# Left-over tokens on full 128-row matmuls, and new priorities, in an attention and token-mixer kernel

## The chip, the cores and the metric

The kernel runs on one core of one Trainium2 chip. The metric is the device time of one execution in microseconds, the median of several runs. The profile is of one execution.

## The reference

Inputs are q, k and v of 4 batches, 8 heads, 576 tokens and 64 channels a head, with a small position bias from a two-layer function of relative position, and the weights of a mixer block.

```
scores = q @ k.T / 8 + bias(i, j, head)       # 576 x 576 for each of 32 heads
attn   = softmax(scores) ; o = attn @ v        # o: 576 x 64 a head
x      = o with the 8 heads side by side       # batch, 576, 512
h      = relu(x.T @ w_tok1) @ w_tok2           # mixes the 576 tokens (256 hidden)
u      = x + h.T
out    = u + relu(u @ w_ch1) @ w_ch2           # mixes the 512 channels (1536 hidden)
```

## The kernel before

**Units.** Attention and token mixing are done for a pair of heads of one batch at a time: 4 pairs x 4 batches are 16 units. Within a unit the 576 queries are cut into 4 chunks of 128 and a left-over of 64. In the fifth chunk the left-over queries of both heads of the pair stand together: head 0 in rows 0 to 63, head 1 in rows 64 to 127.

**A chunk's steps.** *scores* (L666): four float32 products of 64 rows for each head into a PSUM `pair`. *biased* (L670, VectorE): adds the bias and finds the row maximum. *exp* (L684, ScalarE). Then the numerators are turned: *flip* (L703, TensorE transposes of 512 columns into a PSUM `bank`), *flip_hi* (L706, ScalarE) and *flip_lo* (L710, VectorE) write them as two float16 parts, high and low. What is left of a chunk after two flips goes another way: high part, low part on GpSimd, and a DMA transpose on the SP queue (L722). *back* (L746 to L748) multiplies with v: for each head 5 blocks of keys, and for each block three products (high x high, high x low, low x high), so 30 products of 64 or 65 columns. The column of ones beside v gives the sum of each row. *norm* (guard L767, reciprocal L771, division L780) writes chunks 0 and 1, chunks 2 and 3, and the left-over into the tile `x` (128 x 5 x 128), and so frees the PSUM bank of those backs.

**The left-over before.** Its back takes 64 columns of the turned numerators as weights (the head's own half) and writes to 64 PSUM rows: `r`, rows 0 to 63 for an even batch, 64 to 127 for an odd one. So both heads stand side by side on the same 64 rows.

**Token mixing.** When all five parts of `x` are there, they are split into high and low (L308, L323). *mix1* (L796 to L798) is 2 x 5 x 3 products of 128 columns: 5 blocks of tokens, the last with 64 rows. *relu* (L815, L816). *mix2* (L805 to L807) is 5 x 2 x 3 products of 128 columns; the last block has 64 output columns and goes to the rows `r`. Two residual instructions (L819 for 128 x 512, L821 for 64 x 128) add to `x`, and two stores (L825, L827) put the result into DRAM tensors `um` and `ul`.

**Channel mixing.** u is read back in 18 tiles of 128 tokens, turned, and multiplied: *chan1* (L968 to L970) in 5 blocks, *chan2* (L998 to L1000). The 24 weight pieces are loaded as 64-bit words and decoded into two float16 parts on VectorE, GpSimd and ScalarE (L556 to L571) while attention runs and after it.

**What sets the order.** Every step is an entry of a plan: which engines can do it, an estimated cost, what it follows, which buffers it takes and frees. A list scheduler (`Plan.order`) emits the steps: it finds the engine that can start a step first, and among the steps that can start within `SLACK` (0.097) of that moment it takes the one with the smallest due time. Due times are `BASE + 5 * TICK * unit + TICK * chunk + DUE[kind]`. The emitted order is fixed in the program; each engine runs its own part in that order, with waits for what it needs. The bias is made first, in 36 blocks (L423, L425, L441, L447), and goes through DRAM into the buffers from which L670 reads it.

Of the kernel before, what the change touches and what calls it, by code (L numbers as in the profile page):

```python
# [26 lines left out]
NCH = 4  # L27
# [9 lines left out]
TICK = 2.35  # L37
BASE = 67.64
# [16 lines left out]
DUE = {'blk': 29.05,  # L55
       'blkn': 0.67,
       'rect': -81.27,
       'bmm': -146.83,
       'over': -7.76,
       'put': -41.17,  # L60
       'bl': -22.15,
       'bln': 15.56,
       'sums': -79.57,
       'sumsn': 0.87,
       'meas': -52.82,
       'measn': -1.79,
       'measw': 98.18,
       'measwn': 6.48,
       'amax': 56.12,
       'scales': 48.16,  # L70
       'scalet': -63.64,
       'scalec': -167.78,
       'fill': 239.74,
       'fill1': 213.34,
       'tok': 90.83,
       'tokn': 2.6,
       'dec1': 47.92,
       'dec2': -2.25,
       'dec3': -65.12,
       'dec4': 33.12,  # L80
       'dec5': -14.78,
       'load_k': -23.79,
       'load_q': 70.61,
       'load_v': -135.93,
       'prep_k': -68.51,
       'prep_kl': -48.97,
       'prep_q': 82.92,
       'prep_ql': 1.69,
       'prep_v': -126.84,
       'prep_vh': -4.6,  # L90
       'prep_vl': 125.82,
       'scores': 26.19,
       'biased': 82.41,
       'top': 2.07,
       'exp': -41.11,
       'hi': -98.5,
       'lo': -23.53,
       'flip': 29.87,
       'fliphi': 24.58,
       'flip2': 1.74,  # L100
       'fliplo': 11.27,
       'turn': -7.48,
       'back': -24.67,
       'norm': 83.98,
       'mix0': -57.52,
       'mix1': 39.31,
       'relu': -78.51,
       'mix2': -80.52,
       'mix2b': -120.9,
       'store': 48.6,  # L110
       'w1': 22.4,
       'w1n': 11.84,
       'U0': -13.72,
       'U0n': -3.2,
       'U1n': -19.84,
       'U1': -42.9,
       'U2': 133.32,
       'Un': 3.09,
       'U3': 35.03,
       'U4': 250.78,  # L120
       'u1': -106.99,
       'u2': -102.94,
       'u3': 58.75,
       'u4': 8.97,
       'u5': 73.75,
       'G': 114.15,
       'G0': 71.27,
       'G0n': 7.22,
       'g1': -6.35,
       'g2': 90.55,  # L130
       'ur': 190.4,
       'w2m': 20.95,
       'w2mn': 5.39}
# [9 lines left out]
class Step:  # L143
# [5 lines left out]
    def __init__(self, on, due, do, take, free, use, port):  # L149
        key = next(iter(on))  # L150
        self.wire, self.gate = (on[key] if key in "DQX" else 0.0), key == "X"
        on = {"Q": {"A": 0.1}, "X": {"D": 0.0}, "D": {"D": 0.0}}.get(key, on)
        self.on = {e: x if isinstance(x, float) else x[0] for e, x in on.items()}
        self.shy = {e: 0.0 if isinstance(x, float) else self.grid(x[1]) for e, x in on.items()}
        self.due, self.do, self.take, self.free, self.port = self.grid(due), do, take, free, port
        self.bank = [h for h in {*take, *free, *use} if h.kind in ("pair", "bank")]
        self.next, self.left, self.ready, self.start, self.end = [], 0, 0.0, None, None


class Plan:  # L160
# [5 lines left out]
    def add(self, on, due, do, after=(), take=(), free=(), use=(), port=False):  # L166

        s = Step(on, due, do, take, free, use, port)
        for p in after:
            if p is not None:  # L170
                p.next.append(s)
                s.left += 1
        for h in free:
            h.users += 1
        self.steps.append(s)
        return s

    def order(self):
        room = {k: [(0.0, i) for i in range(n)] for k, n in self.rooms.items()}
        at = {"V": 6.9, "A": 6.8, "P": 4.3, "T": 8.0, "D": 2.1, "-": 0.0}  # L180
        made = wire = port = 0.0
        ready = {e: [] for e in at}
# [9 lines left out]
        while len(out) < len(self.steps):  # L192
            best = None
            for e, steps in ready.items():
                first, can = None, []
                for s in steps:
                    t = max(at[e], s.ready, *(h.busy[0] + (0.0 if h.busy[1] == e else 0.15) for h in s.bank))
                    if e == "P" or e == "V" and s.port:
                        t = max(t, port)
                    for h in s.take:  # L200
                        if not room[h.kind]:
                            break
                        t = max(t, min(room[h.kind])[0])
# [17 lines left out]
            cost = s.on[e]  # L221
            s.start, s.engine = t, e
# [27 lines left out]
def attention_mixer(ctx, tc, qT, kT, v, cst, lg, ident, wt1, wt2, wc1, wc2, out, dump=None):  # L250
# [71 lines left out]
    def less(e, o, x, y):  # L322
# [12 lines left out]
           *((wt2[:, a:a + 1, x:x + 288], 288) for a in range(2) for x in (0, 288))]  # L335
# [11 lines left out]
    with tc.manual_schedule():  # L347
# [12 lines left out]
        st["w2"] = [tld.tile([128, 2, S], F16, name="wt2" + x) for x in "hl"]  # L360
# [69 lines left out]
        for n, (c, o) in enumerate([(c, o) for c in range(NCH + 1) for o in range(8 if c < NCH else 4)]):  # L430
# [23 lines left out]
            m = add({"T": 1.15}, t + DUE["bmm"], mm, after=rs, take=[ph], free=[hs])  # L454
# [122 lines left out]
        for i in range(7):  # L577
# [5 lines left out]
            def part(i=i, x=0):  # L583
                a, b = st["w1"][x], st["w2"][x]
                return ((a[:, 0:2], a[:, 2:4], a[:, 4:5], *(b[:, p:p + 1, y:y + 288] for p in range(2) for y in (0, 288)))[i]
# [35 lines left out]
        def unit(u):  # L621
# [6 lines left out]
            r = slice(64 * (b % 2), 64 * (b % 2) + 64)  # L628

# [19 lines left out]
            for c in range(NCH + 1):  # L649
# [4 lines left out]
                for h in range(2 if c < NCH else 1):  # L654
# [20 lines left out]
                    s = lead = chain("scores", add({"T": 0.6 if c < NCH else 0.66}, t + DUE["scores"], scores, after=[*ready, *bias_in[hp, c], lead if h else None], take=[ph, z] if h == 0 else [ph], free=[hk, hq]))  # L675
# [22 lines left out]
                for i in range(groups):  # L698
# [13 lines left out]
                    s = chain("flip", add({"T": 0.51}, t + DUE["flip"] + DUE["flip2"] * i, flip, after=exps[:i + 1], take=[tb, fb], free=[z]))  # L712
# [16 lines left out]
                def back(e, c=c, t2=t2, ta=ta, hb=hb, m=wn // 128):  # L729
# [4 lines left out]
                    if c < NCH:  # L734
                        q = slice(0, 128)
                        blk = [[(n, n) for n in range(5)], [(n + 1, n) for n in range(4, 9)]]
                        w = [slice(0, 128)] * 2
                    else:
                        q = r
                        blk = [[(n + 5 * h, n) for n in range(5)] for h in range(2)]  # L740
                        w = [slice(0, 64), slice(64, 128)]
                    for h in range(2):
                        for i, (n, t) in enumerate(blk[h]):
                            lh, ll = th[t][:, w[h]], tl[t][:, w[h]]
                            o = ps[q, h, 0:D + 1]
                            PE.matmul(out=o, lhsT=lh, rhs=vh[:, n, 0:D + 1], start=(i == 0), stop=False)  # L746
                            PE.matmul(out=ps[q, h, 0:D], lhsT=lh, rhs=vl[:, n, :], start=False, stop=False)  # L747
                            PE.matmul(out=o, lhsT=ll, rhs=vh[:, n, 0:D + 1], start=False, stop=(i == 4))  # L748

                backs.append(chain("back", add({"T": 1.02}, t + DUE["back"], back, after=[*turned_s, v3, *set_ok, *backs[-1:]], take=[hb] if c in (0, 2) else [],  # L750
# [6 lines left out]
                def view(c=c, hb=hb, hr=hr):  # L757
# [4 lines left out]
                    ps = banks[hb.i][r, 320:480].rearrange("p (c h d) -> p c h d", c=1, h=2)  # L762
                    return ps, rc[r, 0:1], x[r, 4:5].rearrange("p c (h d) -> p c h d", h=2), [64, 1, 2, D]
# [9 lines left out]
                def norm3(e, view=view):  # L773
                    ps, rc, xo, sh = view()
                    if e == "A":
                        for i in range(sh[1]):
                            for h in range(2):
                                A.activation(out=xo[:, i, h], in_=ps[:, i, h, 0:D], func=ACTF.Copy, scale=rc[:, i, h])
# [10 lines left out]
            def mix1(e):  # L789
                (w1h, w1l), (xh, xl) = st["w1"], st["xh"]  # L790
                ps = banks[b1.i].rearrange("p (t c) -> p t c", t=4)
                for t in range(2):
                    for c in range(5):
                        p = slice(0, 128) if c < 4 else r
                        w = slice(t * 128, (t + 1) * 128)
                        PE.matmul(out=ps[:, t], lhsT=w1h[p, c, w], rhs=xh[p, c], start=(c == 0), stop=False)  # L796
                        PE.matmul(out=ps[:, t], lhsT=w1h[p, c, w], rhs=xl[p, c], start=False, stop=False)
                        PE.matmul(out=ps[:, t], lhsT=w1l[p, c, w], rhs=xh[p, c], start=False, stop=(c == 4))  # L798

            def mix2(e):  # L800
                (w2h, w2l), (hh, hl) = st["w2"], st["hh"]
                ps, pl = banks[b2.i].rearrange("p (s c) -> p s c", s=4), banks[b1.i][r, 256:384]
                for o, w in [(ps[:, s], slice(s * 128, (s + 1) * 128)) for s in range(4)] + [(pl, slice(512, S))]:
# [10 lines left out]
            s3 = add({"T": 2.1}, t + DUE["mix1"], mix1, after=[s2, *wt_s[:3]], take=[b1], free=[hx])  # L814
# [3 lines left out]
            s6 = add({"T": 1.98}, t + DUE["mix2"], mix2, after=[s5, *wt_s[3:]], take=[b2], free=[hh], use=[b1])  # L818
            s7 = add({"V": 0.67}, t + DUE["mix2b"], lambda e: V.scalar_tensor_tensor(  # L819
                out=x()[:, 0:4], in0=p2(), scalar=c_tm, in1=x()[:, 0:4], op0=ALU.mult, op1=ALU.add), after=[s6], free=[b2])  # L820
            s8 = add({"V": 0.27}, t + DUE["mix2b"], lambda e: V.scalar_tensor_tensor(  # L821
                out=x()[r, 4], in0=banks[b1.i][r, 256:384], scalar=c_tm[r], in1=x()[r, 4], op0=ALU.mult, op1=ALU.add), after=[s6], free=[b1])
# [4 lines left out]
                add(wire("store", 0.09), t + DUE["store"], lambda e: ENG[e].dma_start(out=u_l[b // 2][r, cs], in_=x()[r, 4]), after=[s8], free=[xh_])]  # L827
# [245 lines left out]
def lay_out(q, k, v, w1, b1, w2, moe_w_tok1, moe_w_tok2, moe_w_ch1, moe_w_ch2):  # L1073
    import numpy as np

    def heads(x):
# [24 lines left out]
        "wt1": wt1.transpose(1, 0, 2), "wt2": t2.reshape(2, 128, S).transpose(1, 0, 2),  # L1101
# [18 lines left out]
```

## Time and profile before

| | |
|---|---|
| timed runs | 712.2, 712.88, 715.33 us; median 712.88 |
| span of the profiled execution, first to last instruction | 709.6 us |
| instructions | 16671 |
| TensorE busy | 660.5 us, 93% |
| VectorE, ScalarE, GpSimd busy | 469.2 (66%), 375.0 (53%), 162.9 us (23%) |
| mean granted TensorE clock | 0.990 |

The profiled execution has no separate time of its own beside its span; 712.88 - 709.6 = 3.3 us is what the median holds more. Busy time of an engine counts an instruction from start to end; matmuls overlap, so for TensorE the distance from one start to the next tells more than the duration of one. A tile of TensorE is written rows*columns of the weights: 128*64 is 128 rows and 64 columns.

### The profile page before, as it was taken

What the parts mean: (1) busy time and instruction counts of PE and PEld (TensorE: products, weight loads), DVE (VectorE), ACT (ScalarE), POOL (GpSimd) and SP (SyncE); (2) the same over time, 40 slices, a digit from 0 to 9 for tenths busy, and PEclk for the clock granted to TensorE, in tenths of its full rate; (3) what the DMA queues carried; (4) which work ended last, traced back from release to release, by engine and by line L of the source; (5) the groups of instructions that cost most, each with busy time, mean ns of one, the idle gap of its engine ahead of it and who ended that gap; (6) DMA issues with size and microseconds to landing.
All of it is one profiled execution on the core that took longest, in us unless ns stands there. A gap on an engine that the chain in (4) does not pass through costs nothing. (4 is left out here: it accounts for less than half of the span.)

```text
span 709.6 us, 16671 instructions
## 1 busy us (share of the span) xinstructions
PE 660.5 (93%) x6612; PEld 391.8 (55%) x6612; DVE 469.2 (66%) x1164; ACT 375.0 (53%) x726; POOL 162.9 (23%) x226
## 2 busy tenths in 40 slices
PE   5776779999999999999999999999999999999997
PEld 2322246676667767776767776444444444446443
DVE  5788788987889999999898777579851022112110
ACT  4667769766787787777877653345531022012010
POOL 0121025332354544453323100013430000000000
PEclk9999999999999999999999999999999999999999
DMA  9878867889756596644452248967623220121021
GB/s 337 332 253 284 280 232 224 245 232 242 237 153 181 132 260 182 177 122 115 135 117 61 49 99 213 296 178 183 181 55 120 60 59 1 29 62 29 19 85 31
DMA packets 86814, 111.42 MB, mean 157 GB/s; under 512 B 46928, under 2 KB 56400, under 8 KB 86736
## 3 DMA queue, kind: packets, MB, share of 16 engines
q1 hardware_dynamic: 72048, 70.90, 35.6%
q10 hardware_dynamic: 14688, 39.46, 17.5%
q8 instruction: 52, 0.85, 0.5%
q14 instruction: 26, 0.21, 0.1%
HBM read 80.31 MB, written 20.05 MB: 141 GB/s over the span
## 5 line engine op out<-in xcount | busy, mean ns | idle before, releaser
L666 PE MATMUL pair<-kk,qq 64*128 64x288 f32 (+1 forms) x640 | 107.6, 454 | 8.6 <-DVE mx L670 5.9
L684 ACT ACTIVATE z<-z,mx 128x576 f32<-128x576 f32 x144 | 110.3, 775 | 6.4 <-DVE mx L691 2.6
L670 DVE CUSTOM_DVE_ANT_0 z<-pair,slots 128x576 f32<-128x576 f32 x144 | 108.4, 757 | 7.6 <-PE pair L666 6.2
L710 DVE TENSOR_TENSOR t2a<-bank,t2a 128x512 f16<-128x512 f32 x144 | 98.3, 687 | 16.4 <-ACT t2a L706 16.0
L706 ACT ACTIVATE t2a<-bank 128x512 f16<-128x512 f32 x144 | 84.4, 588 | 42.3 <-PE bank L703 35.6
L703 PE MATMUL bank<-id,z 128*128 128x128 f32 x576 | 92.7, 285 | 4.6 <-ACT z L684 2.9
L1009 DVE SCALAR_TENSOR_TENSOR o<-bank,crow,ur 128x512 f32<-128x512 f32 x18 | 13.5, 751 | 104.2 <-PE bank L1000 104.2
L703 PEld LDWEIGHTS bank<-id,z 128*128 128x128 f32 x576 | 60.8, 141 | 36.8 <-issue 13.6
L746 PE MATMUL bank<-vh,t2a 128*128 128x65 f16 (+1 forms) x704 | 75.7, 196 | 0.7 <-ACT t2a L706 0.7
L746 PEld LDWEIGHTS <-t2a 128*128 128x128 f16 (+1 forms) x704 | 65.0, 99 | 19.6 <-issue 12.3
L747 PE MATMUL bank<-vl,t2a 128*128 128x64 f16 (+1 forms) x704 | 75.0, 193 | 0.0
L748 PE MATMUL bank<-vh,t2a 128*128 128x65 f16 (+1 forms) x704 | 74.6, 194 | 0.0
L968 PE MATMUL bank<-slots 128*128 128x384 f16 (+1 forms) x192 | 67.8, 353 | 0.8 <-DVE t2a L710 0.8
L323 POOL TENSOR_TENSOR p<-z,p 128x128 f16<-128x128 f32 x80 | 36.6, 459 | 138.1 <-ACT p L308 111.5
L970 PE MATMUL bank<-slots 128*128 128x384 f16 (+1 forms) x192 | 67.7, 353 | 0.0
L969 PE MATMUL bank<-slots 128*128 128x384 f16 (+1 forms) x192 | 67.7, 353 | 0.0
L747 PEld LDWEIGHTS <-t2a 128*128 128x128 f16 (+1 forms) x704 | 65.8, 101 | 1.0 <-issue 0.8
L748 PEld LDWEIGHTS <-t2a 128*128 128x128 f16 (+1 forms) x704 | 65.9, 100 | 0.1
L441 PE MATMUL pair<-slots 128*32 128x288 f32 x576 | 48.5, 455 | 14.6 <-ACT slots L447 13.6
L425 DVE TENSOR_SCALAR slots<-slots 128x576 f32<-128x576 f32 x108 | 51.9, 548 | 15.1 <-PE pair L441 14.9
L666 PEld LDWEIGHTS pair<-kk,qq 64*128 64x128 f32 (+1 forms) x640 | 42.8, 175 | 33.8 <-issue 12.4
L990 ACT ACTIVATE ur<-ur,sc 128x512 f32<-128x512 f32 x18 | 13.0, 720 | 79.2 <-DMA ur<-um 65.1
(171 smaller groups left out, 1404.5 us busy)
## 6 DMA issues: line engine op xcount, KB each, us to landing
raw<-wc SPq DMA_DIRECT2D x48, 512.0 KB, 4.4
bd<-slots ACTq DMA_DIRECT2D x36, 288.0 KB, 4.0
kk<-kT ACTq DMA_DIRECT2D x16, 576.0 KB, 5.1
qq<-qT ACTq DMA_DIRECT2D x16, 576.0 KB, 5.9
slots<-bd SPq DMA_DIRECT2D x16, 576.0 KB, 6.1
tv<-v ACTq DMA_DIRECT2D x16, 320.0 KB, 3.6
slots<-v SPq DMA_DIRECT2D x8, 640.0 KB, 11.6
um<-x SPq DMA_DIRECT2D x16, 256.0 KB, 3.4
```

Of the source, the lines that this page charges most:

```text
L666: PE.matmul(out=o[:, n, 0:i], lhsT=qq[w, q0:q0 + m], rhs=kk[w, k0:k0 + i], start=True, stop=True)
L670: V.tensor_tensor_reduce(out=st["z"][z.i][:, o].rearrange("p (n j) -> p n j", n=2), in0=pairs[ph.i][:, :, 0:i], in1=(bias_m[hp][:, c, h, : ...
L684: A.activation(out=zz, in_=zz, func=ACTF.Exp, bias=mx_t[z.i][:, 2 + h:3 + h], scale=0.125)
L703: PE.transpose(banks[tb.i][:, n * 128:(n + 1) * 128], st["z"][z.i][:, 512 * i + n * 128:512 * i + (n + 1) * 128], id32)
L706: A.activation(out=st["t2a"][h.i][:, 0:4].rearrange("p n q -> p (n q)"), in_=banks[tb.i], func=ACTF.Copy)
L710: V.tensor_tensor(out=x[:, 512:1024], in0=banks[tb.i], in1=x[:, 0:512], op=ALU.subtract)
L746: PE.matmul(out=o, lhsT=lh, rhs=vh[:, n, 0:D + 1], start=(i == 0), stop=False)
L747: PE.matmul(out=ps[q, h, 0:D], lhsT=lh, rhs=vl[:, n, :], start=False, stop=False)
L748: PE.matmul(out=o, lhsT=ll, rhs=vh[:, n, 0:D + 1], start=False, stop=(i == 4))
L968: PE.matmul(out=ps[:, 0:n], lhsT=w[0][:, c], rhs=uh[:, c], start=(c == 0), stop=False)
L969: PE.matmul(out=ps[:, 0:n], lhsT=w[0][:, c], rhs=ul[:, c], start=False, stop=False)
L970: PE.matmul(out=ps[:, 0:n], lhsT=w[1][:, c], rhs=uh[:, c], start=False, stop=(c == 3))
```

## The change

The left-over back now takes all 128 columns as weights for each head, so it computes for both heads' queries with each head's v, on 128 PSUM rows; only the block on the diagonal (rows 0 to 63 for head 0, 64 to 127 for head 1) is used. Division, residual and store take the two diagonal blocks one by one. In `x` the fifth part is therefore block-diagonal, with zeros beside it that were written once. mix1 uses all 128 rows of it (the last 64 rows of the first weights stood in both halves already). mix2 computes 128 output rows for the left-over, with the last 64 columns of the second weights put in twice, so that tile is 640 wide in place of 576.

The scheduler now charges `DRAIN` when TensorE goes on to a step of another tile shape, and a refill of 0.055 for flips after one; costs of TensorE's steps are set anew; and all due times, `TICK` and `BASE` are new.

```diff
-TICK = 2.35
-BASE = 67.64
+DRAIN = 0.095
+ROWS64, ROWS64X2, COLS32 = ("64x128", 0.1), ("64x64", 0.1), ("128x32", 0.1)
+TICK = 3.49
+BASE = 15.749
...
-       'put': -41.17,
+       'put': 21.218,
-       'scores': 26.19,
-       'biased': 82.41,
+       'scores': 59.169,
+       'biased': 76.486,
-       'flip': 29.87,
+       'flip': 64.91,
-       'back': -24.67,
-       'norm': 83.98,
+       'back': -707.069,
+       'norm': 410.436,
-       'mix1': 39.31,
+       'mix1': 48.311,
-       'mix2': -80.52,
+       'mix2': -338.728,
-       'w1': 22.4,
-       'w1n': 11.84,
+       'w1': 556.16,
+       'w1n': -19.871,
...
+                    if e == "T" and s.mode != mode:
+                        t = max(t, at[e] + DRAIN)
...
-       for ... in range(2) for x in (0, 288)    # pieces of the second token weights
+       for ... in range(2) for x in (0, 320)
...
-                            lh, ll = th[t][:, w[h]], tl[t][:, w[h]]
-                            o = ps[q, h, 0:D + 1]
-                            PE.matmul(out=o, lhsT=lh, rhs=vh[:, n, 0:D + 1], start=(i == 0), stop=False)
...
+                            o = ps[:, h, 0:D + 1]
+                            PE.matmul(out=o, lhsT=th[t], rhs=vh[:, n, 0:D + 1], start=(i == 0), stop=False)
...
+                    elif c == NCH:
+                        for h, w in enumerate(half):
+                            V.tensor_scalar(out=xo[w, 0, h], in0=ps[w, 0, h, 0:D], scalar1=rc[w, 0, h], scalar2=None, op0=ALU.mult)
...
-                        p = slice(0, 128) if c < 4 else r
-                        PE.matmul(out=ps[:, t], lhsT=w1h[p, c, w], rhs=xh[p, c], start=(c == 0), stop=False)
+                        PE.matmul(out=ps[:, t], lhsT=w1h[:, c, w], rhs=xh[:, c], start=(c == 0), stop=False)
...
-                ps, pl = banks[b2.i]..., banks[b1.i][r, 256:384]
-                for o, w in [... for s in range(4)] + [(pl, slice(512, S))]:
+                ps, pl = banks[b2.i]..., banks[b1.i][:, 256:384]
+                for o, w in [... for s in range(4)] + [(pl, slice(512, 640))]:
...
+            def mixed_left(e):
+                for h, w in enumerate(half):
+                    o = x()[w, 4, 64 * h:64 * h + 64]
+                    V.scalar_tensor_tensor(out=o, in0=banks[b1.i][w, 256 + 64 * h:320 + 64 * h], scalar=c_tm[w], in1=o, op0=ALU.mult, op1=ALU.add)
+            def store_left(e):
+                for h, w in enumerate(half):
+                    ENG[e].dma_start(out=u_l[b // 2][r, hp * 128 + 64 * h:hp * 128 + 64 * h + 64], in_=x()[w, 4, 64 * h:64 * h + 64])
```

## Rows read from the trace of the kernel before

**Rows 1.** Windows: PE, PEld, DVE, ACT, POOL busy us (instructions); clock, DMA share, GB/s.

```profile
0.00:100.00 100.00, 69.05 (x782) 31.90 (x782) 72.71 (x179) 63.43 (x98) 13.49 (x29) 0.93 0.81 285
100.00:200.00 100.00, 92.59 (x1267) 65.31 (x1267) 87.36 (x236) 75.11 (x162) 35.42 (x55) 1.00 0.83 237
200.00:440.00 240.00, 234.81 (x3294) 170.16 (x3291) 213.01 (x553) 173.86 (x365) 91.19 (x119) 1.00 0.54 141
440.00:705.00 265.00, 264.04 (x1275) 124.48 (x1272) 95.38 (x198) 62.63 (x103) 22.77 (x24) 1.00 0.33 95
```

**Rows 2.** TensorE's waits from 200 to 440 us: total, times, longest.

```profile
PE pair L666 <- DVE mx L670: 2.9, 4, 1.4
PE bank L703 <- DVE t2a L710: 0.8, 1, 0.8
PE bank L968 <- DVE t2a L710: 0.8, 1, 0.8
```

**Rows 3.** Timeline of TensorE, mix1 of one unit: start, duration, step.

```profile
247.69 0.23 PE L796 MATMUL bank<-xh,wt1h 128*128 128x128 f16 x1
...
248.31 0.22 PE L798 MATMUL bank<-xh,wt1l 128*128 128x128 f16 x1
248.46 0.23 PE L796 MATMUL bank<-xh,wt1h 64*128 64x128 f16 x1
...
248.58 0.22 PE L798 MATMUL bank<-xh,wt1l 64*128 64x128 f16 x1
248.73 0.23 PE L796 MATMUL bank<-xh,wt1h 128*128 128x128 f16 x1
...
249.78 0.66 PE L703 MATMUL bank<-id,z 128*128 128x128 f32 x4
```

**Rows 4.** The same view, mix2.

```profile
251.97 0.22 PE L805 MATMUL bank<-hh,wt2h 128*128 128x128 f16 x1
...
253.26 0.22 PE L807 MATMUL bank<-hh,wt2l 128*128 128x128 f16 x1
253.41 0.24 PE L805 MATMUL bank<-hh,wt2h 128*64 128x128 f16 x1
...
253.86 0.66 PE L703 MATMUL bank<-id,z 128*128 128x128 f32 x4
```

**Rows 5.** The same view: full back, flip, scores, left-over back, flip.

```profile
217.09 0.20 PE L746 MATMUL bank<-vh,t2a 128*128 128x65 f16 x1
...
218.01 0.63 PE L703 MATMUL bank<-id,z 128*128 128x128 f32 x4
218.57 0.76 PE L666 MATMUL pair<-kk,qq 64*128 64x288 f32 x4
219.26 0.22 PE L746 MATMUL bank<-vh,t2a 128*64 128x65 f16 x1
...
220.20 0.20 PE L748 MATMUL bank<-vh,t 128*64 128x65 f16 x1
220.32 0.66 PE L703 MATMUL bank<-id,z 128*128 128x128 f32 x4
```

**Rows 6.** The same view: the first and the last left-over step.

```profile
112.69 0.22 PE L746 MATMUL bank<-vh,t2a 128*64 128x65 f16 x1
...
439.47 0.22 PE L807 MATMUL bank<-hh,wt2l 128*64 128x128 f16 x1
```

**Rows 7.** Groups of VectorE by form: count, busy us, mean ns, idle before.

```profile
L670 DVE CUSTOM_DVE_ANT_0 z<-pair,slots 128x576 f32<-128x576 f32 x128 | 95.8, 750 | 7.3 <-PE pair L666 6.2 <-POOL vh L310 0.3
L821 DVE SCALAR_TENSOR_TENSOR x<-bank,sc,x 64x128 f32<-64x128 f32 x16 | 5.5, 345 | 0.3
L780 DVE TENSOR_TENSOR x<-bank,rc 64x128 f32<-64x128 f32 x16 | 4.6, 286 | 0.3
L767 DVE TENSOR_SCALAR rc<-bank 64x2 f32<-64x2 f32 x16 | 2.5, 154 | 0.8 <-PE bank L748 0.6
```

**Rows 8.** Left-over store, its issue on SP's queue (min/median/max ns).

```profile
L827 SPq DMA_DIRECT2D ul<-x x16: 456/506/582, 143.9 to 441.1; - x16
```

More of the change, by code (lines that the diff above doesn't have):

```diff
@@ new lines @@
+DUE = {'blk': -301.305,
+       'blkn': 0.445,
+       'rect': -310.123,
+       'bmm': -868.901,
+       'over': -337.858,
+       'put': 21.218,
+       'bl': 40.214,
+       'bln': 12.051,
+       'sums': 94.139,
+       'sumsn': -3.746,
+       'meas': -1082.989,
+       'measn': -255.838,
+       'measw': 304.958,
+       'measwn': 4.395,
+       'amax': 110.376,
+       'scales': -91.311,
+       'scalet': -470.69,
+       'scalec': -264.261,
+       'fill': 31.486,
+       'fill1': -862.237,
+       'tok': 95.732,
+       'tokn': 0.61,
+       'dec1': -52.855,
+       'dec2': -49.699,
+       'dec3': 885.324,
+       'dec4': -448.697,
+       'dec5': -632.954,
+       'load_k': -0.338,
+       'load_q': -59.119,
+       'load_v': -1046.779,
+       'prep_k': -389.112,
+       'prep_kl': -420.883,
+       'prep_q': 720.055,
+       'prep_ql': 159.905,
+       'prep_v': -409.564,
+       'prep_vh': 594.073,
+       'prep_vl': -481.528,
+       'scores': 59.169,
+       'biased': 76.486,
+       'top': -34.795,
+       'exp': 9.644,
+       'hi': -491.185,
+       'lo': -794.221,
+       'flip': 64.91,
+       'fliphi': -27.323,
+       'flip2': -358.745,
+       'fliplo': 89.294,
+       'turn': 1.524,
+       'back': -707.069,
+       'norm': 410.436,
+       'mix0': -1932.907,
+       'mix1': 48.311,
+       'relu': 87.051,
+       'mix2': -338.728,
+       'mix2b': 381.563,
+       'store': 287.708,
+       'w1': 556.16,
+       'w1n': -19.871,
+       'U0': 1242.39,
+       'U0n': 8.843,
+       'U1n': -59.704,
+       'U1': -763.778,
+       'U2': 328.171,
+       'Un': 9.756,
+       'U3': 39.143,
+       'U4': -426.916,
+       'u1': 270.936,
+       'u2': 1707.764,
+       'u3': 188.291,
+       'u4': -926.778,
+       'u5': -397.401,
+       'G': 715.675,
+       'G0': 828.094,
+       'G0n': -31.543,
+       'g1': 280.796,
+       'g2': 350.483,
+       'ur': 589.862,
+       'w2m': 35.422,
+       'w2mn': 18.716}
@@ L710, in flip_lo @@
                         V.tensor_tensor(out=x[:, 512:1024], in0=banks[tb.i], in1=x[:, 0:512], op=ALU.subtract)
-                    s = chain("flip", add({"T": 0.51}, t + DUE["flip"] + DUE["flip2"] * i, flip, after=exps[:i + 1], take=[tb, fb], free=[z]))
+                    s = chain("flip", add({"T": 0.44}, t + DUE["flip"] + DUE["flip2"] * i, flip, mode=(None, 0.055), after=exps[:i + 1], take=[tb, fb], free=[z]))
                     s = chain("hi", add({"A": 0.5}, t + DUE["fliphi"] + DUE["flip2"] * i, flip_hi, after=[s], take=ta[i:i + 1], use=[tb]))
@@ L826, in unit @@
                     after=[s7], free=[xh_]),
-                add(wire("store", 0.09), t + DUE["store"], lambda e: ENG[e].dma_start(out=u_l[b // 2][r, cs], in_=x()[r, 4]), after=[s8], free=[xh_])]
+                add(wire("store", 0.12), t + DUE["store"], store_left, after=[s8], free=[xh_])]
         for u in range(NU):
```

128 lines of the change are left out of this document (31 added, 97 removed).

## The prediction, written before the result was known

> **What bounds the kernel now.** I read the stage table first [rows 1]. From 0 to 100 us TensorE is busy 69.05 us: this is the making of the bias, and nothing is near full (VectorE 72.71, DMA share 0.81). From 100 to 200 it is busy 92.59. From 200 to 440, the steady part of attention and token mixing, it is busy 234.81 of 240, VectorE 213.01, ScalarE 173.86. From 440 on, channel mixing alone, it is busy 264.04 of 265, and nothing in the change touches that. So TensorE sets the pace from about 100 us, with VectorE at 89% as the next in line in the steady part. TensorE's idle time is 31.0 + 7.4 + 5.2 + 1.0 us over the four stages. The waits say the same [rows 2]: in the steady part TensorE waits for VectorE in three places, 4.5 us together, and hardly for anything else. The profiled execution's span is 709.6 us, and the median of the timed runs is 712.88, so 3.3 us lie outside the span; I add them at the end.
>
> A busy TensorE is not yet a TensorE at its peak, so the next view is its timeline, step by step. In mix1 the products follow each other at 0.056 us, but where the rows change from 128 to 64 or back, the distance is 0.15 [rows 3]: 248.31 to 248.46 and 248.58 to 248.73. A third such place follows in mix1, and one at its exit. The surplus is 0.09 to 0.10 us for each change of shape. mix2 shows it with the columns: 253.26 to 253.41 [rows 4], and again at its exit. A left-over back shows it at its exit, 220.20 to 220.32 where 0.03 is usual [rows 5]. The granted clock is 1.00, its higher level, in every stage after 100 us [rows 1], so this is no clock effect.
>
> **The change part by part.** *mix1* takes 2.09 us to the next start (247.69 to 249.78). Thirty products at 0.056 are 1.69: 0.40 less. *mix2* takes 1.89 (251.97 to 253.86) against 30 x 0.056 = 1.68: 0.21 less. *The left-over back* takes 1.06 (219.26 to 220.32), a full one with as many products 0.92 (217.09 to 218.01): 0.14 less, and 0.09 more at its entry, the price of any other change. The number of products stays, and so does their pitch: three 64-row products stand 0.06 apart as the 128-row ones do, so filling the other half costs nothing. That is 0.84 us for a unit, 13.4 for 16. From it comes what remains at the edges. Inside mix1 and mix2 lie 4 changes a unit, 64 in all. The outer edges are 64 more, and I counted over TensorE's timeline, from the first left-over step to the last [rows 6], that only 46 of them vanish; at 18 the neighbour (scores on 64 rows, mostly) has another shape anyway. 18 x 0.095 = 1.7, so 11.7 us of TensorE time go, 110 changes of shape in all. Of the 110, 83 lie after 200 us (8.8 us) and 27 before (2.9 us).
>
> After 200 us TensorE is 98% busy, so I take 8.8 in full. Before, it idles 7% in the stage and other engines finish late as often; the bounds are 0 and 2.9, and I take half, 1.4. Together -10.2.
>
> *VectorE's additions.* The left-over norm is one instruction on 64x128, 286 ns, the left-over residual one, 345 ns [rows 7]; each becomes two on 64x64. No 64x64 instruction is in the trace. The nearest rows are 154 ns for 64x2 and these two, so one lies between 154 and 345; halfway I take about 220 and 250, which makes the pairs 0.15 longer each: 0.3 x 16 = 4.9 us, bounds 0.3 and 9.4. Guard and reciprocal go from 64x2 to 128x2, nothing. This is no term of the sum on its own, since VectorE idles 27 us in the steady part. But the stage is to shrink by 8.8 and VectorE to gain 3.5 there, so its idle time falls from 27 to about 14.7. If TensorE's waits for VectorE, 4.5 us now, grow as that cover thins, they become 4.5 x 27 / 14.7 = 8.3. That is +3.8; bounds 0 and 10. I take +3, since channel work fills TensorE near the stage's end.
>
> *DMA.* The left-over store becomes two. Each issue takes the SP queue 0.51 us [rows 8], so 16 more are 8.1 us of SP over 340 us. Behind one stand the transposes of L722 and the weight loads. In no stage of [rows 2] does TensorE wait long for a transposed tile, so I cost this at nothing; bound, 0.5 a unit, 8. The token weights' second matrix grows from 288 to 320 columns a piece, 11% on four decodes early on, hidden behind the idle time of the first 100 us; bound 0.5.
>
> *The new order.* Every priority changes, and the plan now charges 0.095 for a change of shape. The trace of before can't show the new order. The gain is bounded by idle time before 440 us, 43.6, and by the 287 changes of shape that stay; the loss by the bank rival below, 24. What can be read from the diff is mixed. The offsets that set the steady pace keep their relation: scores stand 3.7 ahead of flip before and 5.7 after, which is 1.6 chunks of the old and of the new TICK. Others invert: norm goes from level with the biased scores to far behind, the first-half weight decode w1 far behind too, back and mix2 far ahead. A few scores steps paired would save two changes each, 0.19 us: at 0.69 for scores and 0.56 for a flip [rows 5], which alternate now, fifteen more pairs are 3 us. I take -3, near zero and on the gaining side because the charge on changes is the one new thing that the order knows.
>
> Sum: -10.2 + 3 - 3 = -10.2. 709.6 - 10.2 = 699.4 in span, 702.7 with the 3.3 outside.
>
> **A rule weighed against the rows.** Four scores products of 288 columns, on 64 rows each, take 0.69 us, while four full flips of 128 columns take 0.56 [rows 5]: half-height tiles do run side by side there. The Trainium skill, TensorEngine Tiling (Array Packing), section Key Properties, says that tiles operate independently and may load and multiply in parallel, with up to twice the speed for a dimension of 64; by that rule going back to the full array gives speed away. In the steps that change, though, the half-size products stand 0.032 to 0.056 apart, just as full ones do [rows 3, 5], since all of a unit's sit in the same half. By the rows nothing is lost; by the rule up to half of 1.6 us a unit, 13 us, would be, and the sum would come out near 716.
>
> **Rivals.** *The bank is held (slower).* norm frees the bank in which the back products of chunks 0 and 2 of the next unit accumulate, and norm is now the last choice of VectorE. A release late by one biased-score instruction (0.750 us [rows 7]) costs up to 0.75; there are 32 releases. From 10 of 32 the gain of the shapes is gone, from 15 it is slower than the measurement's grain. At 24 of 32 it is +18 - 10.2 + 3 = +10.8, 723.7. For it: the offset 410 against 76 for biased. Against: four banks, and VectorE idles 11% in which it takes what is left. *VectorE takes over (no change).* If its cover thins faster than I take, the waits eat the gain: 709 to 716. For it: 89% busy. Against: TensorE waits 4.5 us for it now. *The order wins at the start too (faster).* If a third of the 31 us idle in the first 100 us closes, 10 us more: 693. For it: no engine is full there. Against: the bias chain of VectorE, ScalarE and DMA is unchanged. *The halves did run in parallel,* so that the change gives speed away: the 42 half-size products of a unit take 0.95 + 0.34 + 0.34 us, half of that in 16 units is 13 us, and 702.7 + 13 = 715.7; the pitches of [rows 3, 5] all but exclude it. The Trainium skill's page on tiling, named above, is the rule behind it.
>
> **How the numbers follow.** My forecast (698 to 708) 0.48; start wins (below 698) 0.18; VectorE takes over 0.14; halves in parallel 0.02; bank held 0.18. 702.7 is the time of the first. Half a per cent, 3.6 us, is what a measurement can tell from no change. Faster takes the first two and a little of the third: 0.68; same 0.15; slower 0.17. The range reaches to 688 and 717, leaving out some 0.06 below and 0.13 above; the likeliest alone spans 697 to 708.
>
> **What would show it.** Right: mix1 at 1.7 us, mix2 at 1.7, the left-over back at 0.92 to the next start, no 64-row or 64-column form in them; some 110 fewer changes of shape; the end of attention 8 to 12 us earlier, the channel stage as long as before. Wrong: TensorE's waits for L670, L710 or for banks (behind L780) above 15 us in the steady part; the first 100 us growing longer; a gap before the first channel products, if the weights' decode comes late; or a span that stays although the changes of shape are gone.

## The result, and the profile after

The changed kernel takes 723.44 us (719.45 to 732.05, 4 runs), the kernel before 713.56 (712.2 to 715.33, 4 runs) beside it: 1.0127 times as long, 95% interval 1.0089 to 1.0166. It is slower, by about 9 us, where 10 us less were forecast. The profiled execution is one of 719.45 us with a span of 717.4. A ratio, here and below, leaves out disturbed runs (here that of 732.05 us), so it need not be that of the medians.

The stage table of after, with the columns and stages of [rows 1]:

```profile
0.00:100.00 100.00, 62.12 (x698) 27.36 (x699) 63.61 (x163) 58.22 (x86) 8.64 (x23) 0.88 0.79 273
100.00:200.00 100.00, 86.95 (x1158) 63.53 (x1155) 83.38 (x227) 69.01 (x149) 36.76 (x55) 0.93 0.79 221
200.00:440.00 240.00, 231.34 (x3408) 174.96 (x3407) 214.00 (x581) 185.86 (x392) 91.42 (x124) 1.00 0.56 143
440.00:705.00 265.00, 264.04 (x1322) 126.62 (x1320) 104.23 (x217) 66.11 (x110) 23.17 (x25) 1.00 0.39 104
```

From 200 us on little has changed: TensorE idles 8.7 us of the 240 in place of 5.2, and is as busy as before after that. The loss is ahead of it: TensorE is busy 62.12 us of the first 100 (69.05 before) and 86.95 of the second (92.59), and the granted clock has fallen from 0.93 to 0.88 and from 1.00 to 0.93.

The shapes are as forecast. TensorE's timeline of after, mix1, mix2 and a back:

```profile
228.00 0.22 PE L805 MATMUL bank<-xh,wt1h 128*128 128x128 f16 x1
...
229.62 0.22 PE L807 MATMUL bank<-xh,wt1l 128*128 128x128 f16 x1
229.67 0.19 PE L752 MATMUL bank<-vh,t2a 128*128 128x65 f16 x1
...
231.83 0.23 PE L814 MATMUL bank<-hh,wt2h 128*128 128x128 f16 x1
...
233.51 0.19 PE L752 MATMUL bank<-vh,t2a 128*128 128x65 f16 x1
...
234.43 0.63 PE L714 MATMUL bank<-id,z 128*128 128x128 f32 x4
```

mix1 takes 1.67 us to the next start (2.09 in [rows 3]), mix2 1.68 (1.89 in [rows 4]), a back 0.92, and no 64-row or 64-column form is left in them.

VectorE's groups by form of after, columns as in [rows 7]:

```profile
L788 DVE TENSOR_SCALAR x<-bank,rc 64x64 f32<-64x64 f32 x32 | 9.0, 282 | 0.6
L834 DVE SCALAR_TENSOR_TENSOR x<-bank,sc,x 64x64 f32<-64x64 f32 x32 | 8.9, 279 | 0.5
```

The halves cost 282 and 279 ns in place of the 220 and 250 that I took: 9.0 + 8.9 = 17.9 us against 4.6 + 5.5, so 7.8 more and not 4.9, inside the bounds.

TensorE's waits of after, first from 0 to 100 us, then from 100 to 200, then from 200 to 440 (total, times, longest):

```profile
PE pair L451 <- ACT slots L457: 23.1, 16, 4.4
PE pair L451 <- DVE slots L435: 7.8, 1, 7.8
...
PE pair L677 <- DVE mx L681: 4.1, 1, 4.1
PE bank L714 <- ACT z L695: 3.8, 3, 1.6
...
PE bank L752 <- DMA t<-p: 3.3, 3, 1.7
PE pair L677 <- DVE mx L681: 1.1, 4, 0.4
PE bank L714 <- DVE t2a L721: 1.1, 3, 0.7
PE bank L805 <- DVE t2a L721: 1.1, 1, 1.1
PE bank L814 <- DVE t2a L721: 0.6, 1, 0.6
```

L451 makes the bias products (L441 before). Its waits for ScalarE's L457 are 23.1 us; before, the same view has:

```profile
PE pair L441 <- ACT slots L447: 13.6, 15, 2.2
```

In the steady part no wait is long, and none is behind the late norm. The largest sum, 3.3 us, is for tiles that the DMA transposes (`t<-p`); from 200 to 440 us the trace of before has no such wait.

### The profile page after: what moved, and what is told of

Same layout as the page of the kernel before. It is cut to its first block, busy times and chain, and to the rows that moved or that the text cites. A ratio compares the mean times of both kernels' runs of the same rounds, so it can differ in the third digit from the quotient of the medians.

```text
span 717.4 us, 16776 instructions
## 1 busy us (share of the span) xinstructions
PE 652.2 (91%) x6612; PEld 395.8 (55%) x6612; DVE 466.7 (65%) x1188; ACT 379.2 (53%) x734; POOL 160.0 (22%) x226
## 5 line engine op out<-in xcount | busy, mean ns | idle before, releaser
L681 DVE CUSTOM_DVE_ANT_0 z<-pair,slots 128x576 f32<-128x576 f32 x144 | 108.2, 758 | 14.3 <-PE pair L677 12.6
L721 DVE TENSOR_TENSOR t2a<-bank,t2a 128x512 f16<-128x512 f32 x144 | 97.5, 686 | 8.5 <-ACT t2a L717 7.7
L714 PE MATMUL bank<-id,z 128*128 128x128 f32 x576 | 94.4, 288 | 7.8 <-ACT z L695 4.6
L451 PE MATMUL pair<-slots 128*32 128x288 f32 x576 | 49.0, 471 | 34.4 <-ACT slots L457 23.1
L752 PE MATMUL bank<-vh,t2a 128*128 128x65 f16 x704 | 76.1, 196 | 0.1
L753 PE MATMUL bank<-vl,t2a 128*128 128x64 f16 x704 | 75.9, 194 | 0.0
L754 PE MATMUL bank<-vh,t2a 128*128 128x65 f16 x704 | 75.5, 194 | 0.1
L752 PEld LDWEIGHTS <-t2a 128*128 128x128 f16 x704 | 65.6, 98 | 12.7 <-issue 8.8
L333 POOL TENSOR_TENSOR p<-z,p 128x128 f16<-128x128 f32 x80 | 34.8, 437 | 155.9 <-ACT p L318 137.5
L753 PEld LDWEIGHTS <-t2a 128*128 128x128 f16 x704 | 65.9, 100 | 1.0 <-issue 0.2
L754 PEld LDWEIGHTS <-t2a 128*128 128x128 f16 x704 | 65.9, 98 | 0.3 <-DVE t2a L721 0.2
L435 DVE TENSOR_SCALAR slots<-slots 128x576 f32<-128x576 f32 x108 | 49.4, 519 | 23.6 <-PE pair L451 23.4
L995 ACT ACTIVATE slots<-bank 128x512 f16<-128x512 f32 (+1 forms) x36 | 20.1, 560 | 62.6 <-PE bank L988 62.5
```

The lines of the kernel that those rows point to most:

```text
L681: V.tensor_tensor_reduce(out=st["z"][z.i][:, o].rearrange("p (n j) -> p n j", n=2), in0=pairs[ph.i][:, :, 0:i], in1=(bias_m[hp][:, c, h, : ...
L714: PE.transpose(banks[tb.i][:, n * 128:(n + 1) * 128], st["z"][z.i][:, 512 * i + n * 128:512 * i + (n + 1) * 128], id32)
L721: V.tensor_tensor(out=x[:, 512:1024], in0=banks[tb.i], in1=x[:, 0:512], op=ALU.subtract)
L752: PE.matmul(out=o, lhsT=th[t], rhs=vh[:, n, 0:D + 1], start=(i == 0), stop=False)
L753: PE.matmul(out=ps[:, h, 0:D], lhsT=th[t], rhs=vl[:, n, :], start=False, stop=False)
L754: PE.matmul(out=o, lhsT=tl[t], rhs=vh[:, n, 0:D + 1], start=False, stop=(i == 4))
```

## The experiments

Two theories stood first. **Order:** the edits gain what was forecast and the new due times lose it again, ahead of 200 us. **Edits:** the second instructions and stores, or the larger tiles, cost more than they give. In the diffs, `seq` is the emitted order, `named(kind)` the steps of one kind in it, and `move(s, to)` puts step `s` right behind `to`. Each diff shows only the lines that matter.

**e1_struct and e2_order.** The edits with all costs and due times of before, and the reverse.

```diff
 # e1: before.py and the edits of back, norm, mix1, mix2, residual, store; TICK, BASE, DUE, costs as before
 # e2: after.py and the left-over code of before
```

> The edits alone: left-over back, norm, mix1, mix2, residual and store as in the changed kernel, but every priority, planned cost and thus the emitted order as before the change. Theory A (the new order of the first 130 us loses more than the shapes give): 110 changes of shape go, TensorE's steady part from 200 to 440 us gets about 8 us shorter, and the time is 702 to 706, 8 to 11 under the kernel before. Theory B (the edits themselves cost, on VectorE and in the waits): 713 to 722, no faster than before. Theory C (the edits give nothing, since another engine sets the pace): 710 to 714.

> The order alone: priorities, planned costs and emitted order of the changed kernel, with the 64-row and 64-column left-over of the kernel before. Theory A: the loss of the start without the gain of the shapes, 730 to 735. Theory B: the order is neutral, 710 to 716.

e1: 706.19 us, ratio 0.9912 (0.9883 to 0.9941). e2: 724.97, 1.0176 (1.0142 to 1.0210). The edits gain 6.3 us, the order loses 12.5 on the old code and (1.0127 - 0.9912) x 713 = 15.3 on the new. The Edits theory falls; the order alone costs less than the 730 to 735 that theory A gave. e1 is faster than both kernels, and the fastest that computes the whole reference.

To place the loss I weighted each of TensorE's steps with its usual pitch and summed what was done by each moment, in e1 and in after: after lags by 3.3 us of work at 40 us, 4.9 at 100, 12.0 at 140, 9.2 at 200, about 10 at the end. These are the two profiled executions, e1's slowest and after's fastest, whose spans are 10.0 us apart and not 15.3. In them the loss is complete at 140 us, in two steps, and some comes back. After has 28 fewer changes of shape than e1 (261 against 289), at 0.095 the 2.7 us that I had hoped for.

**e3_start_old and e4_start_new.** One set of due times up to a moment, the other behind it.

```diff
-key=lambda x: x[1].due
+key=lambda x: x[1].due[0 if first < SWITCH else 1]    # SWITCH = 115.0 us of planned time; e4: old and new exchanged
```

> The changed kernel with its edits and planned costs; the scheduler goes by the old due times as long as the planned time is below 115 us, and by the new ones after that. Theory A: the loss is in the start, so bias is done near 87 us and the time is 698 to 707. Theory D (the loss is in the steady order, norm late and backs far behind scores): 715 to 724, as the changed kernel.

> The reverse: new due times up to 115 us of planned time, old ones after. Theory A: the start's loss stays, 718 to 726. Theory D: 700 to 708.

723.72 (1.0149; 1.0118 to 1.0180) and 742.21 (1.0389; 1.0348 to 1.0429). e3 lands where theory D has it; e4 is slower than either theory has it, and D would have had it fast. A switch of priorities makes a third order and not the sum of two: in e3 the first back starts at 102.1 us, later than in both kernels (91.7 before, 99.6 after). So neither tells where the loss is. From here on I took the emitted order as it is and moved single steps.

**The first suspect: stores of the bias issued together.** `put` had become less urgent than the bias steps around it. ScalarE's timeline, before and then after:

```profile
13.25 0.33 ACTq L452 DMA_DIRECT2D bd<-slots  x1
...
15.73 0.33 ACTq L452 DMA_DIRECT2D bd<-slots  x1
...
17.02 0.33 ACTq L452 DMA_DIRECT2D bd<-slots  x1
...
18.83 0.33 ACTq L452 DMA_DIRECT2D bd<-slots  x1
```

```profile
16.68 1.83 ACTq L462 DMA_DIRECT2D bd<-slots  x4
...
23.67 0.74 ACT L457 ACTIVATE slots<-pair,slots 128x576 f32<-128x576 f32 x1 [3.76 <-DMA bd<-slots]
```

After holds the first stores back and issues four in one go; the block that needs the first buffer again waits 3.76 us for it to land, and TensorE behind it 4.40.

**s1_put, s2_sums, s3_put_sums.** s1 sends each of the four stores behind its own block; s2 moves late sums of v and the load ahead of them to an early place; s3 does both.

```diff
+for o, p in list(zip(named("over"), named("put")))[:4]:       # s1, s3
+    move(p, o)
+move(loads[7], loads[6])                                      # s2, s3
+for s in named("sums")[4:] + named("diagonal") + named("scales_v"):
+    move(s, last); last = s                                   # last: at first the 17th bias product step
```

> The changed kernel in its own emitted order, but for four steps: each of the first four stores of bias blocks is issued right behind its eviction, and no longer all four behind the fourth eviction's successors on ScalarE. Theory P (the batched stores stall the bias chain, which waited for their landing from about 20 to 24 us): that wait goes, bias ends 3 to 5 us earlier than 96.7, and the time is 717 to 721 where the changed kernel had 723. Theory Q (the stall is only shifted, since the queues are full of loads): 722 to 725.

> The changed kernel in its own emitted order, but the eighth load of v for its scale is issued right behind the seventh, ahead of the loads that measure the weights, and the four late products of it with the scale behind the 17th bias product. Theory V (the late scale of v, 92.6 us in place of some 44, holds back the first backs and the pipeline behind them from 100 to 140 us): the first back moves from 99.6 to 93 or earlier and the time is 714 to 720. Theory W (backs wait for other things by then): 721 to 725, with the scale early and the rest unmoved.

> Both moves together. If the gains add: 709 to 716. If neither is the cause: 721 to 725.

s1: 717.71, 1.0082 (1.0050 to 1.0113). s2: 728.32, 1.0221 (1.0162 to 1.0279), more than either theory has. s3: 722.25, 1.0160 (1.0105 to 1.0216). The late sums are no cause; moved early they seem to cost, though the intervals just touch. The stores may give 3 us, but the intervals of s1 and of the changed kernel overlap. The bias products of e1, after and s1 (count, ns, first and last start):

```profile
L442 PE MATMUL pair<-slots x576: 402/406/690, 9.5 to 87.6; 128*32 128x288 f32 x192
L451 PE MATMUL pair<-slots x576: 406/406/689, 7.8 to 96.7; 128*32 128x288 f32 x192
L451 PE MATMUL pair<-slots x576: 406/406/690, 7.5 to 93.3; 128*32 128x288 f32 x192
```

The last one starts 9.1 us later in after than in e1. Moving the stores takes back 3.4 of that; no run here traces the other 5.7.

**s4_batch.** The same from the other side: e1 with its first four stores held back as the new order does.

```diff
+for p in named("put")[:4]:      # behind the last ScalarE step ahead of the fifth block
+    move(p, last); last = p
```

> The edits in the old order (the kernel of 706 us), damaged in one place: its first four stores of bias blocks wait, as in the new order, behind the work on ScalarE that precedes the fifth eviction, and go out together. Theory P: ScalarE waits 3 to 4 us for a landing near 20 us, bias ends 3 to 4 us later than 87.6 and the time is 708 to 711. Theory Q: 705 to 707.

713.46, 1.0006 (0.9980 to 1.0032): 0.94%, or 6.7 us, is lost against e1, and the intervals are apart. ScalarE's waits of s4 from 0 to 40 us, beside 0.6 in the kernel before and 4.5 in after:

```profile
ACT slots L448 <- DMA bd<-slots: 4.7, 1, 4.7
```

So the stores are a cause by themselves in the old order. In the new one taking them back gave 3 us, not clear of noise.

**s6_warm.** A rival for the start: the lower clock. Half of each bias block's products are done twice, so that TensorE idles less.

```diff
-for x in range(2):
+for x in (0, 0, 1):
```

> The changed kernel, with the first half of each bias block's products done twice: 36 x 4 products more, some 0.58 us of TensorE for each block, while a pair of blocks takes 3.9 us. Theory K (the lower clock, 37.5 us of the start at half rate against 13.7 before, is itself the loss): half-rate time falls under 15 us and the time is 714 to 719. Theory L (the clock follows the waits and costs little): 722 to 728, whatever the clock does.

732.99, 1.0282 (1.0224 to 1.0340), above both theories. The granted clock of its first 80 us is 0.96 and 1.00 (two halves), and the kernel is still some 11 us slower than after. The repeats add TensorE time of their own to the chain, so this is no price of the clock; but a clock near its higher level does not bring the bias stage's time back.

**The second suspect: the decode of the token weights.** VectorE's timeline of after, the moment when TensorE waits 4.09 us for it; L566, L571 and L581 are the decode, L681 the biased scores:

```profile
114.96 0.33 DVE L566 TENSOR_SCALAR dc<-raw 128x320 int32<-128x320 int32 x1 [0.43 <-POOL dm L573]
115.56 0.65 DVE L581 SCALAR_TENSOR_TENSOR wt2l<-dm,sc,wt2h 128x320 f16<-128x320 f32 x1 [0.27 <-ACT wt2h L574]
116.57 0.49 DVE L571 SCALAR_TENSOR_TENSOR dc<-dm,dc 128x320 int32<-128x320 int32 x1 [0.36 <-POOL dm L568]
118.04 0.58 DVE L566 TENSOR_SCALAR dc<-raw 128x320 int32<-128x320 int32 x1 [0.97 <-POOL dm L573]
118.55 0.81 DVE L681 CUSTOM_DVE_ANT_0 z<-pair,slots 128x640 f32<-128x640 f32 x1
```

```profile
119.42 1.33 PE L677 MATMUL pair<-kk,qq 64*128 64x288 f32 x4 [4.09 <-DVE mx L681]
```

VectorE idles 0.27 + 0.36 + 0.97 = 1.6 of these 3.6 us and yet can't take L681, since a step of the decode that waits for GpSimd or ScalarE stands ahead of it.

**s5_nodec_after, s5_nodec_e1.** Neither loads nor decodes the token weights, in the new order and, as a control, in the old one. The weights are zeros, so token mixing adds nothing.

```diff
+for x in plan.steps[mark:]:     # the token weights' decode
+    x.do = lambda e: None
+s.do = lambda e: None           # and the load
```

> The changed kernel without the loads and the decode of the token weights, which are set to zero at the start instead (token mixing then multiplies by zero weights; all else is computed, in the emitted order). Theory D (the decode, lumped at 100 to 125 us on VectorE ahead of the biased scores, holds up TensorE): the lag behind the old order shrinks, 709 to 716. Theory N: 718 or more.

> The control: the edits in the old order, without the same loads and decode. Theory D: 700 to 706, a gain of at most 6, half of that of the changed kernel or less. Theory N: both gain alike.

In the new order 711.73, 0.9966 (0.9935 to 0.9997), 1.6% or 11.5 us less than the changed kernel. In the old order 705.98, 0.9914 (0.9888 to 0.9940), as e1. The same work, loads and decode, is free in one order and not in the other.

**s7_ahead.** s1, and nine biased scores ahead of the decode on VectorE.

```diff
+if k:                           # p: the biased step; k: decode steps on VectorE between its scores and p
+    seq.remove(p)
+    seq.insert(seq.index(k[0]), p)
```

> The changed kernel with the four stores moved as in the run before, and with nine biased-score steps of the first units put ahead of the token weights' decode steps that stand between them and their scores on VectorE. Theory D: TensorE's 4.4 us wait for a pair near 112 us goes, 711 to 715 where the four stores alone gave 718. Theory N: 716 to 720.

716.89, 1.0065 (1.0035 to 1.0096), hardly under s1. TensorE's timeline of s7:

```profile
110.71 0.76 PE L679 MATMUL pair<-kk,qq 64*128 64x288 f32 x4 [3.62 <-DVE mx L683]
...
117.06 0.24 PE L754 MATMUL bank<-vh,t 128*128 128x65 f16 x1 [4.13 <-DMA t<-p]
```

The wait for the biased scores is 3.62 us where s1 has 4.45, since decode steps that wait for GpSimd or ScalarE still stand ahead of them on VectorE, and a wait for a transposed tile follows. So s7 hardly tests VectorE's queue. GpSimd's and ScalarE's steps of the decode stay early in it too.

**s8_put_nodec, s9_loads_kept.** Both suspects out together; and the decode out with its loads kept.

```diff
 # s8: s1 and s5_nodec_after        # s9: s5_nodec_after without the line that takes out the load
```

> The changed kernel with the first four stores moved as in the store run, and without loads and decode of the token weights (their tiles are zero, so token mixing adds nothing). If stores and decode are the whole of the order's loss, their gains (0.45% and 1.6%) add up and it stands where the edits stand in the old order without decode: 704 to 708 us, ratio 0.988 to 0.994. Rival (the two overlap, or a third part of the order costs as well): 709 to 712, ratio 0.995 to 0.999.

> The changed kernel without the decode instructions of the token weights, whose loads stay (the weight tiles are zero). If the cost is the instructions in the queues of VectorE, GpSimd and ScalarE: as without decode and loads, 709 to 714 us, ratio 0.993 to 1.000. Rival (the loads cost, by their transfers or by their place in SP's queue ahead of the transposes): 718 to 724, ratio 1.006 to 1.015.

s8: 708.36, 0.9940 (0.9913 to 0.9967), within 0.3% of the control in the old order, and the intervals overlap: no third part of the loss is needed. A small one isn't excluded. The last bias product of s8 starts at 93.1 us, 5.4 later than the control's (87.7), and the 2.7 us from fewer changes of shape may hide what that costs. s9: 716.55, 0.9973 (0.9920 to 1.0026). Its six runs spread from 707 to 720 us, so what the loads cost without the decode stays open.

**s10_spread, s11_lump, s12_lump2, s13_batch_lump.** The place of the decode. s10 spreads it in the new order, with the stores as in s1; s11 and s12 put it early in the old one; s13 adds the stores of s4 to s12. The loads of these pieces move with it.

```diff
+for x, n in table:              # load or decode step x goes ahead of scores step n + 1
+    seq.remove(tokens[x])
+    groups.setdefault(n, []).append(tokens[x])
```

> The changed kernel with the first four stores moved as in the store run (which was 1.0082 of the kernel before), and the four pieces of the second token weights (loads and decode) spread over the emitted order: one piece for three scores steps, from the 9th scores step to the 20th. In the changed kernel pieces 3 to 5 all begin between the 8th and the 10th scores step, in the old order between the 16th and the 22nd. Place theory (the order's loss comes from the decode being crowded into the start of attention, on three engines' in-order queues): most of the 11 us that the run without decode gained comes back, 704 to 711 us, ratio 0.988 to 0.998. Rival (the place doesn't matter; the work of the decode has simply no idle time to go into in the new order): 714 to 720, ratio 1.003 to 1.012.

> The edits in the old order (706.2 us, ratio 0.9912), with the pieces of the second token weights crowded as the new order has them: pieces 3 to 6 begin between the 10th and the 13th scores step in place of the 16th to the 25th; nothing else moves. Place theory: half or more of the 11 us are lost here too, 711 to 718 us, ratio 0.998 to 1.008. Rival (crowding costs only together with the rest of the new order): 704 to 708, ratio 0.988 to 0.994.

> The edits in the old order (706.2 us, ratio 0.9912) with the pieces of the second token weights crowded, as in the run before of that kind, but every load now stands ahead of its decode by one or two scores steps and no load is issued into a buffer before the decode has read it (in the run before, one was, so two engines waited 6.6 and 8.3 us for loads and that piece had the wrong content). Pieces 3 to 5 are decoded between the 11th and the 14th scores step, piece 6 at the 17th to the 19th, in place of the 16th to the 28th. Place theory: crowding the decode costs in the old order too, 711 to 717 us, ratio 0.998 to 1.006. Rival (what the run before lost was its waits for loads): 704 to 709, ratio 0.988 to 0.995.

> The edits in the old order, with both things taken over from the new one: the first four stores issued together (that alone was 1.0006 of the kernel before) and the second token weights crowded as in s12. If these two are what the new order lost, the old order now loses as much: 718 to 725 us, ratio 1.007 to 1.017 (the changed kernel is 1.0127). Rival (crowding costs nothing by itself, the new order loses its second part in another way): 710 to 716, ratio 0.997 to 1.004.

s10: 718.43, 1.0076 (1.0041 to 1.0112), a miss: spread over steps 9 to 20 the decode costs as in s1 (1.0082). s11: 719.47, 1.0119 (1.0076 to 1.0161), above its range; in it one load overwrites a piece that was not decoded yet, and engines wait for loads, so it shows little. s12, without that fault: 718.85, 1.0082 (1.0050 to 1.0114), also above its range and 12 us more than e1, by nothing but the place of these loads and decode steps. s13: 723.32, 1.0162 (1.0126 to 1.0198). So two moves in the old order lose as much as the new order lost. s10 and s12 both have the decode ahead of scores step 20, the old order from 16 to 28: what costs seems to be how early it stands and not how dense, but I tried no place later than 20 in the new order. Early is meant against the scores, not in time. VectorE's last step of the second token weights, in e1 and then in after:

```profile
L572 DVE SCALAR_TENSOR_TENSOR wt2l<-dm,sc,wt2h x4: 540/544/785, 123.2 to 138.1; 128x320 f16<-128x320 f32 x4
L581 DVE SCALAR_TENSOR_TENSOR wt2l<-dm,sc,wt2h x4: 540/546/654, 115.6 to 135.7; 128x320 f16<-128x320 f32 x4
```

When the first of the four begins, 88 scores products have begun in e1 and 44 in after; at the last, 124 and 80.

The stretch from 100 to 140 us, in e1, after, s8 and s12 (columns as in [rows 1]):

```profile
100.00:140.00 40.00, 34.41 (x463) 23.18 (x460) 37.58 (x101) 33.62 (x73) 18.34 (x28) 1.00 0.79 238
```

```profile
100.00:140.00 40.00, 30.50 (x310) 20.30 (x309) 29.38 (x78) 27.08 (x60) 17.91 (x27) 0.82 0.74 195
```

```profile
100.00:140.00 40.00, 36.13 (x518) 26.54 (x520) 31.86 (x87) 29.17 (x62) 13.78 (x20) 1.00 0.75 213
```

```profile
100.00:140.00 40.00, 28.05 (x312) 18.51 (x313) 27.82 (x74) 25.02 (x55) 15.53 (x23) 0.79 0.61 189
```

With the decode early TensorE does 310 matmuls in place of 463 to 518, VectorE and ScalarE are less busy too, and the clock is 0.82 or 0.79 in place of 1.00. What a step of the decode waits for is not the same in both: in after GpSimd and ScalarE, in s12 mostly a load, as VectorE's waits of s12 from 95 to 140 us show:

```profile
DVE dc L557 <- DMA raw<-wt: 5.4, 2, 4.3
```

## Why the prediction was wrong

The failed step is **the new order**, "I take -3". It cost 12.5 us alone and 15.3 with the edits, inside my bounds (24 lost, 43.6 gained) but on the other side. Its reason, fewer changes of shape, was right: 28 fewer, 2.7 us. What I didn't price is the start. I read the offsets of the steps that set the steady pace and called the rest mixed; `put` stood in the diff, from -41 to +21, and I gave it no sentence. Held back as in the new order, the first four stores alone cost 6.7 us in the old one (s4). The token weights' decode I called "hidden behind the idle time of the first 100 us", by its size. That was a misreading of the trace of before, where VectorE's last steps of it come later:

```profile
L571 DVE SCALAR_TENSOR_TENSOR wt2l<-dm,sc,wt2h x4: 509/512/629, 122.1 to 136.8; 128x288 f16<-128x288 f32 x4
```

Most of it runs from 95 to 135 us in the timeline of after too. Its place in the order costs 12 us in the old order (s12), and leaving it out with its loads gives 11.5 in the new one (s5). Why an early place costs so much is argued from the waits, not shown: a step that waits holds up what stands behind it in its queue. So the 31 us idle in [rows 1] were not only room to gain, as the rival "the order wins at the start" had it; a worse order added to them, 37.9 us in after.

**The transposed tiles.** The store term I put at nothing since TensorE waited for no transposed tile. In after it waits 4.9 us for them from 100 to 440 us, 0.2 before. In e1, with the second stores, it is 1.0, so most of it comes with the new order. s8 has 6.0 and is within 0.3% of its control, so no run shows that these waits cost.

**The edits** came out as forecast, within the interval. -10.2 for the shapes and +3 for VectorE's cover, -7.2 together, stand against -6.3 (-8.3 to -4.2). 397 changes of shape became 289, 108 fewer where I counted 110. How the 6.3 divide between the two terms isn't measured. The steady part of e1, with the columns of [rows 1]:

```profile
200.00:440.00 240.00, 233.16 (x3346) 172.63 (x3345) 218.50 (x587) 175.68 (x371) 91.59 (x119) 1.00 0.56 144
```

VectorE is busy 218.50 of 240 us (213.01 before), and TensorE's idle time is 6.8 in place of 5.2, so some of the gain did turn into waits, 1.6 us and not 3.8.

**The halves in parallel.** Had the half-size products run side by side, the edits would have cost time. They gain. The Trainium skill, TensorEngine Tiling (Array Packing), section Key Properties, says that different tiles can load weights and multiply in parallel. No run here shows that for these products, which all sat in the same half of the array for a unit; after the change a back's 30 products take 0.92 us, as a full back's did before.

**The bank is held.** This rival's time, 723.7, came out, and its cause didn't: TensorE's waits of 200 to 440 us in after name no norm (L788, L790). A right number isn't a right reason. What I had listed as the sign of a wrong forecast, the first 100 us growing longer, is what happened.

**VectorE takes over.** Not borne out: in the steady part of after TensorE's waits for L681 and L721 add up to 3.9 us, where [rows 2] have 4.5.

**The channel stage** is as long as before. The last left-over product of after, where [rows 6] have 439.47:

```profile
448.50 0.22 PE L816 MATMUL bank<-hh,wt2l 128*128 128x128 f16 x1
```

From there to the end of the span it is 268.9 us, 270.1 before. So attention ends 9 us later and not 8 to 12 earlier.

## What to carry to other kernels

Read a change of priorities at its start first, where no engine is full and steps wait for one another: list which DMA issues and which side jobs change places with the chain's own steps. Test an order by moving single steps in what was emitted, from both sides (undo in the new, do in the old); a mix of two sets of priorities is a third order. Separate the edit from the retuning that comes with it: here the edit alone gains 0.9%, and retuned it loses 1.3%.

## What the runs showed of the hardware that I had not expected

Four stores held back and issued together, in place of one by one, cost 6.7 us of 706 in the old order, with one wait of 4.7. A late start isn't simply carried to the end, though: the last bias product of s8 starts 5.4 us later than the control's, and the kernel takes 1.9 us more, an amount within noise.

The granted clock fell behind idle stretches here, and it shows within a step. TensorE's timeline of after, a back behind waits of 1.04 and 1.22 us:

```profile
109.97 0.66 PE L714 MATMUL bank<-id,z 128*128 128x128 f32 x4 [1.22 <-ACT z L695]
...
110.82 0.20 PE L752 MATMUL bank<-vh,t2a 128*128 128x65 f16 x1
110.85 0.22 PE L753 MATMUL bank<-vl,t2a 128*128 128x64 f16 x1
110.88 0.24 PE L754 MATMUL bank<-vh,t2a 128*128 128x65 f16 x1
110.94 0.24 PE L752 MATMUL bank<-vh,t2a 128*128 128x65 f16 x1
110.99 0.24 PE L753 MATMUL bank<-vl,t2a 128*128 128x64 f16 x1
```

The distance of starts goes from 0.03 to 0.055, the lower of the two levels (1.2 for 2.4 GHz). If all time below 1.00 is at that level, the first 200 us hold 2 x (12 + 7) = 38 us of it in after and 2 x 7 = 14 before. In s6, whose repeats add work, a higher clock did not shorten the bias stage. What the lower one adds to the loss from 100 to 140 us, where TensorE has 0.82 over 40 us, was not separated from the waits that come with it. TensorE idles 9.5 us there in after and 5.6 in e1, while the lag grows by 7.1; so some 3 us of that lag, by this estimate, are not idle time, and slower products may be their source. This stays open.
